# The first batch of a threshold-attention and SwiGLU kernel, issued by a planner, with k and q turned on TensorE

## The chip, the cores and the metric

The kernel runs on one core of one Trainium2 chip. The metric is the device time of one execution in microseconds (us); a profile lists every instruction of one execution, with times from the start of its span. The engines are named as in the profile: PE (TensorE; PEld is its weight load), DVE (VectorE), ACT (ScalarE), POOL (GpSimd) and SP (SyncE, which here only starts DMAs).

## What is computed

Attention with a threshold instead of a plain softmax, for 8 batches of 8 heads, 576 tokens and 64 numbers per head, and a SwiGLU block behind it, all in fp32:

```python
scores = scale * np.matmul(q, k.transpose(0, 1, 3, 2))
thresh = np.max(scores, axis=-1, keepdims=True) - tau
scores = np.where(scores >= thresh, scores, -1000000000.0)
scores = scores - np.max(scores, axis=-1, keepdims=True)
attn = np.exp(scores)
attn = attn / (np.sum(attn, axis=-1, keepdims=True) + 1e-09)
x = (attn @ v), heads side by side          # 4608 tokens x 512
g = x @ w_gate; silu = g * (1.0 / (1.0 + np.exp(-g)))
out = (silu * (x @ w_val)) @ w_out          # 512 -> 1536 -> 512
```

The three weight matrices come as 64-bit floats, 512 x 1536 twice and 1536 x 512.

## The kernel before

Work is cut by batch and by pair of heads (two heads side by side are 128 rows, 32 pairs in all). The kernel has two parts with different forms.

**The first batch** (pairs 0 to 3) is worked in tiles of 128 queries. There are 20 tiles: for each pair first the tiles 0 and 1 (here called early tiles, 8 in all), then, pair by pair in the order 3, 0, 1, 2, the tiles 2, 3 and the half tile 4 of 64 queries (the late tiles, 8 full and 4 half). A tile goes through `scores` (lines 454 to 505), `flip_steps` (514 to 549) and `attend_tile` (551 to 569):

- PE multiplies q by k for both heads into PSUM (`sc`, L463, L469 for half tiles). DVE takes the maximum (L480), ACT makes the threshold (L483, once per head) and the exponential (L484), DVE masks with the threshold and sums (L487), adds and inverts the sum (L489, L490).
- p is then divided by its sum and transposed by PE in blocks of 128 keys (`tp`, and `end` for the last 64 keys). In early tiles ACT multiplies a unit matrix by the reciprocal (L503) and PE multiplies p by this diagonal (L533, L537), which transposes and scales at once. In late tiles p itself is scaled, one head by ACT (L497) and the other by POOL (L495), and PE transposes with the plain unit matrix (L531, L539, L543).
- ACT copies the transposed p out of PSUM (L540, L544, L547), PE multiplies it by v (`xa`, L564, L566), and ACT copies the result (L569) to x.

The tile loop (766 to 824) is a pipeline written by hand: scores of tile n, then the product with v of tile n-2, then the flip of tile n-1, then other work. q and k of the pairs are loaded as blocks of 32 numbers (`load_qk`, L399), turned within 32 x 32 blocks by DVE (`prepare`, L693, L697, and L749 for the rest of q), and q is scaled before that (L403 on POOL, L696 on DVE for the first pair).

Beside the tiles the weights are converted from 64-bit words to fp32 in 24 pieces (16 of the gate and value matrices, 8 of the output matrix), each with a DMA (L314, L311), two ACT operations (L330 for the upper words, L331 for the lower), a clamp on POOL (L323), a shift and a join on DVE (L350, L356) and an addition on POOL (L366). And "plain" groups, the products of x with the gate and value weights without further tricks, fill PE: four groups of the first 256 tokens are done here (`gate`, `value`, L580; each 16 products of 128 x 128 x 256), with a multiplication on POOL (L611).

What is issued where in this part is written out by hand. `STARTS` lists the first DMAs, and `STEPS` names, for a tile by its pair and place and for a point in it, which step of the weights or of q and k is issued:

```python
STEPS = {
    (0, 0, "flipped"): ("qk",),
    (0, 1, "maxima"): ("prepare",),
    (0, 1, "masked"): ("split",),
    ...
```

**The rest** (28 pairs) runs in slots: each slot has the scores of a third of a pair (`slot_scores`, L1776) and their softmax (`slot_rest`, L1797 to L1852), every third slot a product with v (`attend`, L1873), and between them PE runs the gate, value and output products (`plain_group` L1251, `Group.mul` L1047, `outputs` L1326 and others). Their order comes from `Plan` (lines 28 to 109): every operation outside PE is a job with an engine, an estimated time, the jobs it depends on and a rank; PE's work is issued in program order with `pe`, which advances a clock `plan.t`, and whenever the clock moves, the jobs whose engine would be free are issued, lowest rank first. So the order of the instructions on each engine is fixed when the kernel is built. `PLAIN` says how many quarters of plain groups go into the slots 0 to 7, and `rest_of_weights` (905 to 944) puts the pieces not converted by then into the plan.

Of the kernel before, what the change touches and what calls it, by code (L numbers as in the profile page):

```python
# [10 lines left out]
F32 = mybir.dt.float32  # L11
# [16 lines left out]
class Plan:  # L28
# [84 lines left out]
STARTS = ("weights", "v", "weights", "qk", "weights", "v", "v", "weights")  # L113

STEPS = {
    (0, 0, "flipped"): ("qk",),
    (0, 1, "maxima"): ("prepare",),
    (0, 1, "masked"): ("split",),
    (0, 1, "end"): ("scale",),
    (1, 0, "flipped"): ("split", "shift"),  # L120
    (1, 0, "masked"): ("join",),
    (1, 1, "flipped"): ("weights 2", "prepare"),
    (1, 1, "masked"): ("split", "shift"),
    (1, 1, "end"): ("join",),
    (2, 0, "maxima"): ("rest", "weights 2"),
    (2, 0, "flipped"): ("rest",),
    (2, 0, "masked"): ("shift", "scale", "split", "join"),
    (2, 0, "end"): ("weights 2",),
    (2, 1, "maxima"): ("scale", "prepare", "v", "rest"),
    (2, 1, "flipped"): ("rest", "split"),  # L130
    (3, 0, "flipped"): ("shift",),
    (3, 0, "end"): ("join",),
    (3, 1, "maxima"): ("shift", "split", "turn last"),
    (3, 1, "flipped"): ("weights 2", "scale", "prepare"),
    (3, 1, "masked"): ("split",),
    (3, 1, "end"): ("turn", "shift", "scale"),
    (4, 0, "flipped"): ("turn", "qk"),
    (4, 1, "maxima"): ("scale",),
    (4, 1, "masked"): ("scale",),
    (4, 2, "end"): ("turn",),  # L140
# [4 lines left out]
def kernel(  # L145
# [55 lines left out]
    minus2 = const.tile([P, 1], F32, name="minus2")  # L201
    nc.vector.memset(minus2, -2.0)
# [50 lines left out]
    dbufs = deque(room(2 * P).rearrange("p (h q) -> p h q", h=2) for _ in range(2))  # L253
# [27 lines left out]
    wpieces = deque()  # L281
# [16 lines left out]
    NW = len(wpieces)  # L298
    fetched, split, used = deque(), deque(), set()
    joined = []  # L300

    def fetch_weights(n=1):
        for _ in range(n):
            if not wpieces or wpieces[0][2] in used:
                return
            dst, srcs, place = wpieces.popleft()
            used.add(place)
            m = 2 if len(srcs) == 2 else nf
            to = places[place].bitcast(U64).rearrange("p (m n) -> p m n", m=m)
            if len(srcs) == 1:  # L310
                nc.sync.dma_start(out=to, in_=srcs[0])  # L311
            else:
                for x, src in enumerate(srcs):
                    nc.sync.dma_start(out=to[:, x, :], in_=src)  # L314
            fetched.append((dst, place))

    def words(place, dst, w):
        return places[place].bitcast(U32).rearrange("p (m n w) -> p m n w", m=dst.shape[1], w=2)[:, :, :, w]

    early_slots, clamped, unclamped, shifted, unsummed = [True], [], deque(), [], []  # L320

    def clamp(eng, x):
        eng.tensor_scalar(out=x, in0=x, scalar1=1.875 * 2.0 ** -80, scalar2=2.0 ** -111, op0=ALU.min, op1=ALU.max)  # L323

    def split_weights():
        if fetched:
            dst, place = fetched.popleft()
            lo = los[0].rearrange("p (m n) -> p m n", m=dst.shape[1])
            los.rotate(1)
            nc.scalar.activation(dst, words(place, dst, 1).bitcast(F32), AF.Abs, scale=2.0 ** -96)  # L330
            nc.scalar.activation(lo, words(place, dst, 0), AF.Identity, bias=minus2, scale=-2.0 ** -51)  # L331
            unclamped.append(dst)
            if early_slots[0]:
# [1802 lines left out]
```

## Time and profile before

| What | Value |
|---|---|
| runs, median (lowest to highest) | 1362.62 us (1360.74 to 1362.79), 3 runs |
| the profiled execution | 1360.49 us |
| its span, first to last instruction | 1358.7 us |
| granted clock, mean | 1.000 |
| busy: DVE, ACT, POOL | 1065.5, 879.5, 634.8 us |
| first scores of the first batch (L463) | 7.89 us |
| third, ninth tile's scores | 16.56, 47.92 us |
| first slot's scores (L1776) | 128.80 us |
| first product with v of a slot (L1873) | 167.73 us |

The durations used below are those of the profiled execution. A row of a view with "x16" counts records: a product of fp32 operands leaves two records on PE (and two weight loads), a plain transpose one. Two instructions of one engine that follow each other can overlap by their tails, so spacing from start to start says more of PE's throughput than a mean duration. In the waits, "A <- B" means that A's engine stood idle until B ended.

### The profile page before, as it was taken

What the parts mean: (1) busy time and instruction counts of PE and PEld (TensorE: products, weight loads), DVE (VectorE), ACT (ScalarE), POOL (GpSimd) and SP (SyncE); (2) the same over time, 40 slices, a digit from 0 to 9 for tenths busy, and PEclk for the clock granted to TensorE, in tenths of its full rate; (3) what the DMA queues carried; (4) which work ended last, traced back from release to release, by engine and by line L of the source; (5) the groups of instructions that cost most, each with busy time, mean ns of one, the idle gap of its engine ahead of it and who ended that gap; (6) DMA issues with size and microseconds to landing.
All of it is one profiled execution on the core that took longest, in us unless ns stands there. A gap on an engine that the chain in (4) does not pass through costs nothing.

```text
span 1358.7 us, 39214 instructions
## 1 busy us (share of the span) xinstructions
PE 1345.4 (99%) x15590; PEld 1114.5 (82%) x15590; DVE 1065.5 (78%) x2815; ACT 879.5 (65%) x2280; POOL 634.8 (47%) x662
## 2 busy tenths in 40 slices
PE   9999999999999999999999999999999999999998
PEld 7777877887788788877887788887887788999998
DVE  7788898878887777777778777877787766788786
ACT  6888777777756767677766776777767673330330
POOL 2687497543455569324952387326932492000000
PEclk9999999999999999999999999999999999999999
DMA  8753324545425531654154514552255404424411
GB/s 187 196 183 102 73 60 136 166 132 143 140 48 162 146 92 41 190 145 114 37 172 130 157 30 136 157 141 72 65 165 145 114 27 146 155 79 146 158 60 32
DMA packets 208295, 162.33 MB, mean 119 GB/s; under 512 B 166128, under 2 KB 180464, under 8 KB 202736
## 3 DMA queue, kind: packets, MB, share of 16 engines
q1 hardware_dynamic: 204192, 158.90, 41.4%
q8 instruction: 124, 2.03, 0.6%
q10 hardware_dynamic: 3920, 0.92, 0.3%
q14 instruction: 59, 0.48, 0.1%
HBM read 138.28 MB, written 21.50 MB: 118 GB/s over the span
## 4 chain that ended last, share of the span: by engine, by line
PE 93%; DVE 3%; DMA 1%; POOL 1%; issue 0%; ACT 0%; SPq 0%; ACTq 0%; DVEq 0%; POOLq 0%
PE pb L1047 18%; PE pa L1047 12%; PE px L1529 12%; PE sc L1776 10%; PE xa L1873 9%; PE pe L1047 9%; PE po L1326 5%; PE py L1538 5%; PE pg L1251 2%; PE pv L1251 2%; PE sc L1208 2%; PE sc L463 1%; PE xa L564 1%; PE tp L533 1%; PE pe L1208 1%; PE pv L580 1%
## 5 line engine op out<-in xcount | busy, mean ns | idle before, releaser
L1824 DVE SCALAR_TENSOR_TENSOR pall<-sc,th,pall 128x288 f32<-128x288 f32 x504 | 243.9, 514 | 62.8 <-ACT pall L1822 46.1
L1047 PE MATMUL pb<-xall,big 128*128 128x256 f32 x1152 | 273.4, 380 | 0.0
L1822 ACT ACTIVATE pall<-sc,nm 128x288 f32<-128x288 f32 x504 | 231.9, 496 | 38.7 <-DVE pall L1824 38.7
L1047 PEld LDWEIGHTS pb<-xall,big 128*128 128x128 f32 x1152 | 216.9, 190 | 30.3 <-issue 2.2
L1852 DVE STREAM_TRANSPOSE pall<-pall 128x576 f32<-128x576 f32 x252 | 186.8, 761 | 29.1 <-ACT pall L1850 21.1
L1850 ACT ACTIVATE pall<-pall,ri 128x288 f32<-128x288 f32 x418 | 191.7, 527 | 24.1 <-DVE ri L1838 23.6
L1047 PE MATMUL pa<-xall,big 128*128 128x256 f32 x768 | 183.6, 382 | 0.0
L900 POOL TENSOR_TENSOR hall<-hall,tmp 128x512 f32<-128x512 f32 x80 | 102.5, 1281 | 161.2 <-DVE hall L1100 143.3
L1797 DVE TENSOR_REDUCE mx<-sc 128x2 f32<-128x576 f32 x168 | 125.5, 747 | 47.7 <-PE sc L1776 47.1
L1047 PEld LDWEIGHTS pa<-xall,big 128*128 128x128 f32 x768 | 143.2, 190 | 22.1 <-issue 3.6
L1776 PE MATMUL sc<-kT,qT 64*32 64x288 f32 (+1 forms) x5376 | 145.7, 346 | 0.9 <-issue 0.9
L1776 PEld LDWEIGHTS sc<-kT,qT 64*32 64x32 f32 x5376 | 95.6, 106 | 53.7 <-issue 19.3
L1047 PE MATMUL pe<-xall,big 128*128 128x256 f32 x576 | 137.3, 382 | 0.1
L1873 PE MATMUL xa<-pall,vall 64*32 64x288 f32 x4032 | 129.3, 404 | 0.0
L1047 PEld LDWEIGHTS pe<-xall,big 128*128 128x128 f32 x576 | 108.7, 190 | 16.9 <-issue 2.6
L1873 PEld LDWEIGHTS xa<-pall,vall 64*32 64x32 f32 x4032 | 74.1, 107 | 47.5 <-issue 6.2
L1832 ACT COPY sums<-sums 32x6 f32<-32x6 f32 x336 | 66.6, 198 | 32.4 <-DVE pall L1824 27.4
L1847 POOL TENSOR_SCALAR pall<-pall,ri 128x288 f32<-128x288 f32 x86 | 42.5, 506 | 92.6 <-DVE ri L1838 92.0
L1099 ACT ACTIVATE vall<-tmp 128x512 f32<-128x512 f32 x96 | 60.1, 629 | 31.3 <-POOL tmp L900 14.4
L900 POOL TENSOR_TENSOR tmp<-tmp 128x512 f32<-128x512 f32 x36 | 45.9, 1275 | 62.6 <-ACT tmp L1122 62.5
L1799 DVE TENSOR_REDUCE mx<-sc 128x1 f32<-128x288 f32 x168 | 75.0, 446 | 0.0
L1538 PE MATMUL py<-wo,hall 128*128 128x256 f32 x336 | 74.8, 379 | 0.0
(258 smaller groups left out, 2438.3 us busy)
## 6 DMA issues: line engine op xcount, KB each, us to landing
big<-sums_hbm SPq DMA_DIRECT2D x42, 1024.0 KB, 5.2
big<-sums_hbm SPq DMA_DIRECT2D x48, 768.0 KB, 4.8
vall<-in_v_dram SPq DMA_DIRECT2D x112, 144.0 KB, 3.1
out_dram<-big SPq DMA_DIRECT2D x32, 256.0 KB, 2.9
qT<-in_q_dram SPq DMA_DIRECT2D x112, 72.0 KB, 4.7
kT<-in_k_dram SPq DMA_DIRECT2D x112, 72.0 KB, 3.0
wo<-in_moe_w_gate_dram SPq DMA_DIRECT2D x16, 384.0 KB, 3.8
wo<-in_moe_w_val_dram SPq DMA_DIRECT2D x16, 384.0 KB, 4.5
```

The lines of the kernel that those rows point to most:

```text
L900: return lambda: nc.gpsimd.tensor_tensor(out=out, in0=a, in1=b, op=op)
L1047: nc.tensor.matmul(ps[:, i], w[:, k_, i * P:(i + 1) * P], x[:, k_, :], start=first and i == k_ == 0, stop=True, skip_group_check=True)
L1529: nc.tensor.matmul(ps, a[:, f, :], ws[n][:, f, :], start=bank_ not in begun, stop=True, skip_group_check=True)
L1538: nc.tensor.matmul(ps(), a[:, f, i * P:(i + 1) * P], operands[o][:, f, :], start=first and f == 0, stop=True, skip_group_check=True)
L1776: nc.tensor.matmul(pss[h][(slice(g * G, (g + 1) * G), *part)], qT[hs, col:col + G], kT[hs, c * SH + keys[0]:c * SH + keys[1]], start=True, ...
L1797: rs.append(job("DVE", 0.72, lambda n=n, tile_=tile_: nc.vector.tensor_reduce(out=mx[:, n:n + 2, 0], in_=tile_[:, :, 0:SH], axis=AX.X, op= ...
L1799: rs.append(job("DVE", 0.42, lambda n=n, tile_=tile_: nc.vector.tensor_reduce(out=mx[:, n + 2:n + 3, 0], in_=tile_[:, :, SH:SH + SQ], axis ...
L1822: ej = job("ACT", 0.42, lambda x=x, n=n: nc.scalar.activation(ps[x], scs[x], AF.Exp, bias=nm[:, n:n + 1]), ej, masks.get((h, u - 1)), rank=0)
L1824: masks[x] = job("DVE", 0.45, lambda x=x, n=n: nc.vector.scalar_tensor_tensor(out=ps[x], in0=scs[x], scalar=th[:, n:n + 1], in1=ps[x], op0 ...
L1850: scaled.append(job("ACT", 0.46, lambda x=x, n=n: nc.scalar.activation(x, x, AF.Copy, scale=ri[:, n:n + 1]), rj, rank=rank))
L1852: seg["turned"].append(job("DVE", 0.72, lambda both=both: nc.vector.transpose(out=both, in_=both), *scaled, rank=rank))
L1873: nc.tensor.matmul(holds[a].ap()[x * G:(x + 1) * G, 0:SH].rearrange("d (i q) -> d i q", q=G), vr[rs, h, j, ds], p[rs, h, :, j, :], start=( ...
```

## The change

The hand-written order of the first batch goes: `STEPS`, the tile loop with its points, `fetch_weights`, `split_weights`, `shift_weights`, `join_weights`, `need`, `fill`, `rest_of_weights`. `Plan`, `Bank` and `Hold` are made ahead of the first batch, and every operation of it is now a job with an estimate; `convert` makes the six jobs of a weight piece. PE's program is still one loop: scores of tile n, the extra steps that `HOOKS` names for it, the product with v of tile n-2, the flip of tile n-1, and `feed`, which adds quarters of plain groups until the account says that the masks of the tile are done. It feeds three groups; the fourth goes to slots 0 and 1, where `PLAIN` now has 6 quarters each instead of 3 and 5.

The parts that touch the arithmetic's form:

- k and q of the first batch are loaded in whole rows of 64 numbers, 128 tokens per block, and turned by PE with the unit matrix: seven transposes for each pair's k and first 256 queries (`prepare_pair`), three for the rest of q (`prepare_rest`). ACT copies them out of PSUM and scales q in the copy.
- All p of the first batch is scaled by POOL (L507 of the new kernel), both heads; ACT no longer scales p, and there are no diagonals. All flips are plain transposes (L535, L548). The keys of the second head start 64 later in every tile, so `scores` has five products in early tiles too.
- ACT makes one threshold per tile, between the two exponentials.
- The clamp of the weights is always on POOL, and the constants of the conversion differ (`plus2`, no scaling of the upper words).

```diff
-STARTS = ("weights", "v", "weights", "qk", "weights", "v", "v", "weights")
-STEPS = {
...
+STARTS = (("weights", 0), ("v", 0), ("weights", 1), ("qk", 2), ("weights", 2), ("v", 1), ("v", 2), ("weights", 3), ("qk", 3), ("v", 3))
+EARLY_PATIENCE = 0.6
+HOOKS = {
+    1: (("qk", 1), ("load", 3)),
+    2: (("load", 0),),
...
+    8: (("next", 4),),
+    10: [("rest", 0)] + [("weights", n) for n in range(16, 24)],
...
+    def convert(n, *deps):
...
+        fj = job("SP", 0.45 * len(srcs), fetch, *freed.get(place, ()), *deps, rank=1, lag=1.6, moves=2.4)
...
+        uj = job("ACT", 0.9, lambda: nc.scalar.activation(dst, up, AF.Abs), fj, *under, rank=2)
+        cj = job("POOL", 0.85, lambda: clamp(dst), uj, rank=2)
+        lj = job("ACT", 1.0, lambda: nc.scalar.activation(lo, words(place, dst, 0), AF.Identity, bias=plus2, scale=2.0 ** -51),
+                 fj, *conv[-3:-2], rank=2)
...
+        conv.append(job("POOL", 1.85, lambda: nc.gpsimd.tensor_tensor(out=ub, in0=ub, in1=lo.bitcast(U32), op=ALU.add), jj, lj, rank=2))
...
+        rj = job("DVE", 0.36, total, *masks, rank=1)
+        scaled = [job("POOL", 0.8, lambda x=x: nc.gpsimd.tensor_scalar(out=ps[x], in0=ps[x], scalar1=ri[:, x:x + 1], scalar2=1.0,
+                                                                       op0=ALU.mult, op1=ALU.mult), rj, rank=1) for x in range(m)]
...
+            def turn_keys(hold=hold, p=p, h=h):
+                tp = hold.ap()
+                for kt in range(KT):
+                    at_ = kt * P + (D * h if t < NT else 0)
+                    nc.tensor.transpose(tp[:, kt * P:(kt + 1) * P], p[:, at_:at_ + P], ident)
+            m = pe(0.45, turn_keys, *hold.deps, scaled[h])
...
+    def prepare_pair(i):
...
+        m = pe(0.45, keys, *hold.deps, landed[i, "k"])
+        kj = job("ACT", 0.53, lambda: nc.scalar.copy(kTs[i][:, 0:KM], hold.ap()), m, rank=0)
...
+        ej = job("ACT", 0.2, lambda: nc.scalar.copy(kTs[i][:, KM:S], more.ap()[:, QA:QA + D]), m, rank=0)
+        qj = job("ACT", 0.33, lambda: nc.scalar.activation(qT[:, 0:QA], more.ap()[:, 0:QA], AF.Copy, scale=scl), m, rank=0)
...
+    def feed():
+        plan.force(*last_masks)
+        until = max(j.end for j in last_masks) + 0.8
+        while fed[0] < 4 * NF2 and plan.t < until:
...
+    for n in range(len(tiles)):
+        scores(n)
+        if not n:
+            pe(1.9, lambda: run_idle(4))
+        for what, i in HOOKS.get(n, ()):
...
+        if n > 1:
+            attend_tile()
+        if n:
+            flip()
+        feed()
...
-    PLAIN = {0: 3, 1: 5, 2: 6, 3: 2, 4: 5, 5: 5, 6: 3, 7: 3}
+    PLAIN = {0: 4, 1: 6, 2: 6, 3: 2, 4: 5, 5: 5, 6: 3, 7: 3}
+    PLAIN[0] += 2 * 4 * NF2 - fed[0] - sum(PLAIN.values())
```

## The prediction

> **What bounds the kernel now.** First the page's busy line: PE is busy 99% of the span. That line cannot show a stall of half a microsecond, because the modelled end of a matmul covers it, so I split the first 168 us by stage. From PE's 160th group of instructions on (the first `xa` of L1873, at 167.73 us) the two kernels issue the same 870 groups on PE, and the list of PE's waits after 128 us holds almost nothing (0.6 us before a `pg` of L1251, 0.9 us before `sc` of L1776). So the change is worth what it does to the time of that one `xa`.
>
> ```profile
> PE 1345.4 (99%) x15590; PEld 1114.5 (82%) x15590; DVE 1065.5 (78%) x2815; ACT 879.5 (65%) x2280; POOL 634.8 (47%) x662
> ```
>
> Busy time by stage: length, then PE, PEld, DVE, ACT and POOL in us, the granted clock, DMA.
>
> ```profile
> 16.56:47.92 31.36, 31.29 (x276) 25.24 (x276) 28.75 (x63) 30.94 (x72) 15.12 (x14) 1.00 0.81 196
> 69.58:89.45 19.87, 18.52 (x141) 14.26 (x140) 15.94 (x31) 17.60 (x35) 15.57 (x11) 1.00 0.49 158
> 89.45:109.20 19.75, 18.59 (x143) 14.32 (x142) 15.74 (x30) 17.64 (x35) 16.32 (x11) 1.00 0.47 159
> 128.80:167.73 38.93, 38.35 (x437) 31.07 (x443) 34.02 (x92) 29.84 (x75) 18.28 (x19) 1.00 0.42 91
> ```
>
> The reader is to see three regimes. The first row holds the early tiles (two of each pair): ACT is busy 99%, DVE 92%. Rows two and three hold one period each of the late tiles (two full tiles, one half tile, one plain group): ACT 89%, POOL 78 to 83%, PE 93%. The last row is the first four slots: PE alone. PE's waits up to 128 us point at softmax and POOL:
>
> ```profile
> PE sc L463 <- DVE pall L487: 2.8, 4, 1.1
> ...
> PE tp L531 <- POOL big L323: 0.4, 1, 0.4
> ```
>
> **The change, part by part.** PE's pieces come from the chain of waits (start, us, what):
>
> ```profile
> 24.72 1.95 PE tp L533 x16
> 26.67 0.37 PE end L537 x4
> ...
> 119.11 0.88 PE tp L531 x8
> 119.98 0.11 PE end L539
> ...
> 128.87 1.65 PE sc L1776 x64
> ...
> 167.73 4.53 PE xa L1873 x144
> ```
>
> *Plain transposes.* An early flip now multiplies p by a diagonal, and each fp32 matmul leaves two records: 1.95 + 0.37 us. A plain transpose leaves one: 0.88 + 0.11. Eight early flips: 8 x 1.33 = 10.6 us off PE. Their scores are cut in five instead of four products: ten records take 1.30 us (69.58 to 70.88) against 1.18 (22.03 to 23.21), 8 x 0.12 = 1.0 us on.
>
> *k and q by TensorE.* 40 transposes of 0.104 us (0.83 / 8) are 4.2 us; they come in 12 blocks, each with a lead-in that the trace shows as 0.17 to 0.38 us between unlike blocks, say 0.2: 2.4 us. One pair's 0.9 us falls before the first scores. On: 5.7 us. PE's content falls by 10.6 - 1.0 - 5.7 = 3.9 us. By content it was 8 early tiles x 4.94 (22.03 to 26.97), 8 late x 3.8, 4 half tiles x 2.9, 128 plain products (55.2, with lead-ins 57.6) and 4 slot scores x 1.65: 145.7 us, of the 159.8 between the first scores (7.89) and 167.73. So 14 us are waits today, 4 of them in the first two tiles and 8 to 9 in the late ones. Both numbers are the room.
>
> *ACT.* It loses 16 diagonals of L503 (0.35 us each in a row of two), 12 scalings of L497 (0.81) and 16 of 36 thresholds (about 0.2): 5.6 + 9.7 + 3.2 = 18.5 us. It gains the copies of transposed k and q; with the rows of ACT's copies of such widths (512 columns 0.55, 128 columns 0.27) a pair costs 0.55 + 0.25 + 0.4 and its rest 0.4: 6.4 us for four. *DVE* loses the transposes of L693, L697 and L749 and one scaling, 3.0 + 1.6 + 2.0 + 0.35 = 7 us. *POOL* loses 3.6 us of scaling q and gains 28 scalings of p at 0.9 us, 25 us. Three POOL and two ACT rows:
>
> ```profile
> 24.20 1.82 POOL L366 TENSOR_TENSOR big<-big,extra 128x768 uint32<-128x768 uint32 x1
> ...
> 97.54 0.89 POOL L495 TENSOR_SCALAR pall<-pall,ri 128x576 f32<-128x576 f32 x1 [0.37 <-DVE ri L490]
> ...
> 99.30 2.52 POOL L366 TENSOR_TENSOR big<-big 128x768 uint32<-128x768 uint32 x1
> ...
> 29.38 0.70 ACT L503 ACTIVATE pall<-pall,ri 128x128 f32<-128x128 f32 x2
> ...
> 109.85 0.84 ACT L497 ACTIVATE pall<-pall,ri 128x576 f32<-128x576 f32 x1
> ```
>
> The same addition takes 1.82 or 2.52 us, the clamp of L323 0.83 or 1.53, each 0.70 longer when DVE is at its weights. The Trainium skill ("SBUF — State Buffer", section "SBUF: two separate sides") calls the port pair that GpSimd and VectorE share an exclusive lock, held for a whole instruction; these two-valued rows agree. By that rule the new scalings are blocked too, each by at most one such 0.70.
>
> *Start.* k and q arrive in rows of 64 numbers instead of 32, with fewer and larger packets; k landed at 5.7 us. But ACT issued its last start DMA only when an earlier one had landed, then loaded its table (1.28 us from 6.63), and now the copies of k and q queue behind that: 6.4 + 0.6 + 0.25 + 0.4 gives 7.7 for the first scores against 7.89. Bounds: 1.5 us earlier, 1 us later. The first softmax then sets the pace, with scores of the third tile at 16.5 as now: POOL's 0.9 for L503's 0.7 in front of the first flip, and DVE's transposes (1.2) in the second tile replaced by ACT's copies (1.2).
>
> *Early tiles.* ACT has 1.45 (two exponentials, one threshold) + 1.5 (copies) + 0.6 (k, q) + 0.9 (only half a weight piece per tile in the new order) = 4.4; DVE 3.5 + 0.8 = 4.3; PE 3.8 + 0.5 = 4.3; POOL 1.8 + 1.3. Two of six tiles have 1.1 us of copies between the two exponentials, in front of the masks. Four at 4.4, two at 5.4: 28.4 us, so the ninth tile's scores start at 45.0, now 47.9. Bounds: 42.1 (PE alone) and 47.9.
>
> *Late tiles.* The new order feeds three plain groups, not four, here; the fourth (16 products, 6.9 us) moves into the first two slots. The first three tiles carry none: 3 x 4.1 = 12.4 us, by DVE and PE. Then three periods. PE's content is 17.8 + 0.55 (rest of q) = 18.35. POOL: now 15.6 to 16.3 of 19.7 with two scalings; five make 18.3 to 19.0. ACT 17.6 - 1.6 - 0.6 + 0.4 = 15.8. POOL becomes the fullest, and each flip waits for it. I take 20.0 for a period, the nearest row being today's 19.6 to 19.9 with ACT that full; bounds 18.35 and POOL with every weight operation in its long form, 5 x 0.94 + 4 x (1.53 + 2.52) + 1.98 = 22.9. Slots start at 45.0 + 12.4 + 60.0 = 117.4, now 128.8.
>
> *Slots.* 38.9 us today for 64 products; 80 make 45.8. About five pieces of weights instead of two are joined here, some 10 us more of POOL (18.3 of 38.9 busy today) and 5 of DVE (34.0): cover enough. If it is not, PE waits a few us for masks. The sums of weights end later too, but `po` of L1326 used them at 215.8, 27 us after they were ready. SP issues fewer DMAs for k and q, and no transfer is late in either stage.
>
> **Sum.** 117.4 + 45.8 = 163.2 against 167.7: 4.5 us gained, and I add 0.5 for PE's wait of 0.6 us in the first slot, which goes: 5.0. The profiled execution took 1360.49 us (span 1358.7 and 1.8 around it); less 5.0 that is **1355.5**. The median shown is 1362.62, 2.1 above that execution, so against the median the same sum reads 1357.6.
>
> **Rivals.** *PE dense:* the new order, all on one account, runs like the slots, which wait for nothing at DVE 87%. Early tiles 4.3, periods 18.35: 42.1 + 11.2 + 55.1 + 45.8 = 154.2, 13.5 gained: 1347. Against: flips follow their softmax by 2 to 3 us, slots by 10.
> *Nothing left:* the early loop stays at 5.3 through its latency, POOL takes ACT's place: 47.9 + 12.4 + 60 + 45.8 = 166.1, 1.6 gained: 1359. For: the three engines end within 5% of each other.
> *Slower:* POOL in front of every late flip. Scaling queues behind a 2.52 us addition on an in-order engine, and the transposes stand on PE ahead of the plain products that could fill. At 22.9 a period the three cost 8.7 more than in my sum: 1364.2. It decides from 21.7 a period, where my gain is used up. Against: in most periods today half the additions are short.
> *Clock:* transposes might not count as work for the clock. 112 more of them at twice 0.104 us would add 11.6 us: 1367. The rows against it: 80 transposes ran at 0.104 us and the granted clock is 1.00 in every stage. The Trainium skill ("TensorE: Matmul & The Clock Gate", section "Part 4: PE-mode transpose") says that the full clock does not engage for transposes; no row here shows that.
>
> **Chances.** Forecast 0.42 (its own range 1352 to 1358), PE dense 0.22, nothing left 0.22, slower 0.11, clock 0.03. A measurement of this kernel tells about 0.2% (2.7 us) from no change, so faster means below 1357.8. Faster: 0.39 + 0.22 + 0.04 = 0.65; slower: 0.01 + 0.09 + 0.03 = 0.13; the same 0.22. The range, 1346 to 1364, leaves out half the slower case, the clock, and the far end of PE dense.
>
> **What would show it.** The first slot scores (L1551) start near 117 and the first `xa` of L1648 near 163; early tiles follow at 4.4 to 5.4; transposes keep 0.104 us and clock 1.00; POOL is over 90% busy in the late tiles and ends PE's waits before `tp`. I am wrong if the early loop stays at 5.3, if PE waits in the first slots, or if POOL's scalings take much over 0.9.

## The result, and the profile after

Five runs of the changed kernel: 1367.84 us median (1366.24 to 1368.69), against 1362.62 (1360.65 to 1363.20) of the kernel before on the same chip: ratio 1.0042, 95% interval 1.0027 to 1.0057. It is slower by 0.4%, some 5 us; the forecast was 1355.5 (1357.6 beside the median). The profiled execution took 1367.84 us (span 1366.0, mean granted clock 0.994); that of the kernel before lies at the fast end of its runs (1360.49), so between the two profiles the difference is 7.3 us.

The page's busy line has not moved, and the stages have. First that line, then the view by stage (length, then PE, PEld, DVE, ACT, POOL, granted clock, DMA), here the early tiles, the three late periods, and the slots up to the first `xa` of L1648:

```profile
PE 1346.7 (99%) x15550; PEld 1115.9 (82%) x15550; DVE 1072.2 (78%) x2800; ACT 873.5 (64%) x2252; POOL 656.4 (48%) x685
```

```profile
15.99:45.08 29.09, 28.72 (x240) 22.92 (x240) 25.00 (x55) 25.63 (x57) 15.90 (x18) 1.00 0.62 157
58.07:77.14 19.07, 18.54 (x145) 14.00 (x144) 15.98 (x26) 15.93 (x33) 13.01 (x12) 1.00 0.72 248
77.14:102.47 25.33, 21.90 (x144) 16.49 (x143) 19.85 (x36) 16.91 (x32) 19.25 (x15) 0.87 0.44 128
102.47:126.04 23.57, 20.29 (x141) 15.01 (x141) 19.02 (x32) 15.99 (x31) 22.25 (x18) 0.86 0.18 65
126.04:175.72 49.68, 45.61 (x461) 37.27 (x461) 46.85 (x102) 38.58 (x86) 34.44 (x28) 1.00 0.49 119
```

The early tiles are faster than before. One late period is good (19.1 us), the next two take 25.3 and 23.6 us, with a granted clock of 0.87 and 0.86, where the kernel before had 1.00. In the slots VectorE is busy 46.9 of 49.7 us. The list of PE's waits (us in total, times, longest) has three new entries at its head:

```profile
PE end L548 <- ACT xlast L577: 4.1, 2, 3.0
PE xa L1648 <- issue: 3.5, 1, 3.5
PE xa L570 <- DVE hall L623: 2.3, 1, 2.3
```

The rows of PE's timeline that answer to those shown of before (start, us, what): a plain flip, the first slot, the first `xa` of the slots.

```profile
99.61 1.10 PE L535 MATMUL tp<-pall 128*128 128x128 f32 x8
...
126.04 1.72 PE L1551 MATMUL sc<-kT,qT 64*32 64x288 f32 x64
...
175.72 0.84 PE L1648 MATMUL xa<-pall,vall 64*32 64x288 f32 x6 [3.46 <-issue]
```

The first `xa` starts at 175.72 instead of 167.73, 8.0 us later; the span is 7.3 us longer. So nothing more was lost behind it, and all of the loss lies ahead of it.

**Where it was lost.** The second late period shows it. VectorE's timeline, then GpSimd's, then PE's:

```profile
73.88 2.16 DVE L398 TENSOR_SCALAR big<-big 128x768 uint32<-128x768 uint32 x1 [0.72 <-POOL big L371]
76.08 1.46 DVE L400 SCALAR_TENSOR_TENSOR big<-wo,big 128x768 uint32<-128x768 uint32 x1
77.46 0.80 DVE L496 SCALAR_TENSOR_TENSOR pall<-sc,th,pall 128x576 f32<-128x576 f32 x1
...
78.58 1.27 DVE L398 TENSOR_SCALAR big<-big 128x768 uint32<-128x768 uint32 x1
79.89 1.38 DVE L400 SCALAR_TENSOR_TENSOR big<-wo,big 128x768 uint32<-128x768 uint32 x1
81.19 0.67 DVE L623 SCALAR_TENSOR_TENSOR hall<-tmp,pv 128x512 f32<-128x512 f32 x1
81.79 1.41 DVE L489 TENSOR_REDUCE nm<-sc 128x1 f32<-128x576 f32 x2
```

```profile
73.81 1.81 POOL L402 TENSOR_TENSOR big<-big 128x768 uint32<-128x768 uint32 x1
75.60 1.13 POOL L371 TENSOR_SCALAR big<-big 128x768 f32<-128x768 f32 x1
77.62 1.81 POOL L402 TENSOR_TENSOR big<-big,extra 128x768 uint32<-128x768 uint32 x1 [0.89 <-DVE big L400]
79.53 0.93 POOL L507 TENSOR_SCALAR pall<-pall,ri 128x576 f32<-128x576 f32 x1
```

```profile
77.14 2.54 PE L467 MATMUL sc<-pall 64*128 64x288 f32 x10
82.01 1.97 PE L570 MATMUL xa<-big,vall 128*64 128x128 f32 x16 [2.33 <-DVE hall L623]
```

The shift of a weight piece (L398) takes 0.54 us when GpSimd stands. Here it begins 0.07 us behind an addition of GpSimd (73.81 to 75.62), takes 2.16 us and ends 0.42 us after that addition. The shift at 78.58 takes 1.27 us and again ends 0.42 us after GpSimd's addition. The join (L400) goes from 0.95 to 1.38 and 1.46. So one side stands still while the other runs. The masks of L496, whose scores lie in PSUM, keep 0.81 us throughout. Two conversions now stand in VectorE's queue ahead of the gate's product (L623), which PE's `xa` waits for. The Trainium skill ("SBUF — State Buffer", section "SBUF: two separate sides") says that an instruction of VectorE with two SBUF inputs or in a two-port mode, and one of GpSimd, exclude each other as a whole. These rows agree.

The other two long waits begin on VectorE too. Its rows, ScalarE's and PE's ahead of the wait of 3.0 us, then VectorE's last transposes of p ahead of the first `xa` of the slots:

```profile
112.05 1.30 DVE L400 SCALAR_TENSOR_TENSOR big<-wo,big 128x768 uint32<-128x768 uint32 x1
113.28 1.41 DVE L489 TENSOR_REDUCE nm<-sc 128x1 f32<-128x576 f32 x2
...
114.06 0.74 ACT L491 ACTIVATE pall<-sc,nm 128x576 f32<-128x576 f32 x1 [2.23 <-DVE nm L489]
116.02 0.21 ACT L577 COPY xlast<-xa 128x64 f32<-128x64 f32 x1
...
116.29 0.47 PE L548 MATMUL end<-pall 128*128 128x128 f32 x1 [3.02 <-ACT xlast L577]
...
174.21 1.41 DVE L1627 STREAM_TRANSPOSE pall<-pall 128x576 f32<-128x576 f32 x2
```

Two joins and a shift (110.11 to 113.35) stand ahead of the maxima at 113.28. ScalarE's exponential waits 2.23 us for these, the copy L577 stands behind it on ScalarE, and PE waits for the copy. For the first `xa` of the slots the list names no releaser; in the kernel that product depends on the transposes of L1627, and the last of them ends at 175.62, 0.1 us ahead of it. Two shifts and a join of weights (168.08 to 171.56), and maxima behind these, stand ahead of them on VectorE.

Then comes a second price. The same 16 records of `xa` take 1.09 us at 103.77 and 1.97 here. The stages in steps of half a microsecond show where (the granted clock is the third number from the end):

```profile
80.50:81.00 0.50, 0.00 (x0) 0.00 (x0) 0.50 (x1) 0.00 (x0) 0.00 (x0) 0.53 1.00 406
87.00:87.50 0.50, 0.50 (x3) 0.41 (x2) 0.39 (x1) 0.50 (x2) 0.50 (x1) 0.65 0.00 0
```

The clock is at 0.50 from 80.53 to 87.35, from 114.66 to 121.49 and from 176.10 to 179.5 (a mean of 0.53 over half a microsecond is 0.50 from 0.03 us on), and each stretch begins in or just behind one of the three long waits.

### The profile page after: what moved, and what is told of

It reads as the page before. It is cut to its first block, busy times and chain, and to the rows that moved or that the text cites. A ratio compares the mean times of both kernels' runs of the same rounds, so it can differ in the third digit from the quotient of the medians.

```text
span 1366.0 us, 39121 instructions
## 1 busy us (share of the span) xinstructions
PE 1346.7 (99%) x15550; PEld 1115.9 (82%) x15550; DVE 1072.2 (78%) x2800; ACT 873.5 (64%) x2252; POOL 656.4 (48%) x685
## 3 DMA queue, kind: packets, MB, share of 16 engines
q1 hardware_dynamic: 196304, 158.90, 40.9%
q8 instruction: 123, 2.02, 0.6%
## 4 chain that ended last, share of the span: by engine, by line
PE 93%; DVE 5%; issue 1%; ACT 1%; DMA 0%; POOL 0%; SPq 0%; DVEq 0%; ACTq 0%; POOLq 0%
PE pb L861 18%; PE pa L861 12%; PE px L1304 12%; PE sc L1551 10%; PE xa L1648 9%; PE pe L861 9%; PE po L1101 5%; PE py L1313 5%; PE pv L602 2%; PE pg L602 2%; PE sc L1022 2%; PE sc L467 1%; DVE big L400 1%; PE pe L1022 1%; DVE pall L496 1%
## 5 line engine op out<-in xcount | busy, mean ns | idle before, releaser
L1627 DVE STREAM_TRANSPOSE pall<-pall 128x576 f32<-128x576 f32 x252 | 186.8, 761 | 29.8 <-ACT pall L1625 22.0
L359 POOL TENSOR_TENSOR hall<-hall,tmp 128x512 f32<-128x512 f32 x84 | 108.1, 1287 | 158.8 <-DVE hall L914 141.8
L1648 PE MATMUL xa<-pall,vall 64*32 64x288 f32 x4032 | 130.7, 408 | 3.5 <-issue 3.5
L1648 PEld LDWEIGHTS xa<-pall,vall 64*32 64x32 f32 x4032 | 77.0, 108 | 49.4 <-issue 9.1
```

What stands on the lines that cost most here:

```text
L359: return lambda: nc.gpsimd.tensor_tensor(out=out, in0=a, in1=b, op=op)
L1627: seg["turned"].append(job("DVE", 0.72, lambda both=both: nc.vector.transpose(out=both, in_=both), *scaled, rank=rank))
L1648: nc.tensor.matmul(holds[a].ap()[x * G:(x + 1) * G, 0:SH].rearrange("d (i q) -> d i q", q=G), vr[rs, h, j, ds], p[rs, h, :, j, :], start=( ...
```

## The experiments

Times are medians beside the kernel before on the same chip. PE starts cold in some executions (last section), so stages are counted from the ninth tile's scores. "Late" is from there to the first slot, "slots" from there to the first `xa` of the slots. The number of plain products in each of the two differs where the order differs, so the sum is what compares. The kernel before took 1361.1 to 1361.6 us (medians) on the chips of the experiments; the ratio is over all executions, so that a single one that is some us longer draws it away from the ratio of the medians.

| kernel | late, us | slots, us | sum | time, us | ratio to before (interval) |
|---|---|---|---|---|---|
| before | 80.9 | 38.9 | 119.8 | 1362.62 | 1 |
| forecast | 72.4 | 45.8 | 118.2 | 1357.6 | |
| changed | 81.0 | 49.7 | 130.6 | 1367.84 | 1.0042 (1.0027 to 1.0057) |
| keep_clock | 76.9 | 51.2 | 128.1 | 1365.70 | 1.0043 (1.0025 to 1.0060) |
| no_dve_weights | 69.5 | 45.0 | 114.5 | 1348.90 | 0.9908 (0.9894 to 0.9923) |
| no_pool_scale | 73.3 | 49.7 | 123.1 | 1361.42 | 1.0002 (0.9993 to 1.0012) |
| no_add_scale | 69.6 | 47.2 | 116.8 | 1356.45 | 0.9962 (0.9948 to 0.9976) |
| act_head0 | 62.8 | 75.8 | 138.6 | 1375.04 | 1.0100 (1.0085 to 1.0115) |
| dve_scale | 64.4 | 78.3 | 142.7 | 1380.98 | 1.0144 (1.0129 to 1.0159) |
| true_account | 65.5 | 66.3 | 131.8 | 1366.98 | 1.0047 (1.0029 to 1.0064) |
| lock_plan | 56.9 | 87.5 | 144.4 | 1382.56 | 1.0154 (1.0139 to 1.0169) |
| xlast_first | 65.3 | 62.9 | 128.2 | 1366.61 | 1.0047 (1.0029 to 1.0065) |
| late_wo | 79.1 | 49.4 | 128.5 | 1368.28 | 1.0039 (1.0024 to 1.0053) |
| late_wo_clock | 76.9 | 50.5 | 127.4 | 1364.90 | 1.0027 (1.0016 to 1.0037) |
| ep2 | 83.0 | 48.2 | 131.2 | 1368.47 | 1.0051 (1.0036 to 1.0066) |
| ep2_late | 81.5 | 48.1 | 129.6 | 1368.00 | 1.0050 (1.0033 to 1.0066) |
| before_pool_all | 83.3 | 39.8 | 123.1 | 1365.30 | 1.0026 (1.0017 to 1.0035) |
| before_plain | 81.0 | 39.0 | 120.0 | 1361.14 | 0.9998 (0.9989 to 1.0007) |

The theory at the start: VectorE comes late because its weight operations run long beside GpSimd's, and the clock doubles the price of each long wait. The rivals: GpSimd with all scalings is itself too full; ScalarE's queue order; the account's durations; the clock falls because of the transposes.

**keep_clock: is it the gap that takes the clock?**

```diff
-            marks.append(pe(..., (lambda h=h: one(h)) if full else both_heads, *deps))
+            marks.append(pe(..., (lambda h=h: one(h, 4 if h and k == 14 else 1)) if full else both_heads, *deps))
...
-                for kt in range(KT):
+                for kt in list(range(KT)) * (7 if h and len(flipped) == 18 else 1):
...
-                for c in range(NCC):
+                for c in list(range(NCC)) * (2 if (t, g, mat, i) == (1, 1, 1, 1) else 1):
```

> Same order on every engine as the changed kernel; only in the three stretches in which PE stood for about 3 us (before the xa of tile 12, before the end of tile 17, before the first xa of the slots) the matmuls just before are issued again into the same bank: second head of the 15th tile's scores four times, one flip's four transposes seven times, one plain product twice. More work on PE, nothing less. Theory 'gap, then half clock': the granted clock stays 1.00 through 180 us, slots start at 119 to 121 instead of 126.0, first xa of the slots near 169 instead of 175.7, time 1360 to 1362. Rival 'the clock falls for another reason (transposes, load)': drops to 0.66 to 0.83 stay, time 1368 or a little more.

PE's timeline, the repeated scores, and the two stages:

```profile
77.04 5.80 PE L467 MATMUL sc<-pall 64*128 64x288 f32 x28
```

```profile
44.98:121.85 76.87, 74.44 (x581) 57.67 (x581) 65.75 (x117) 59.17 (x117) 60.47 (x50) 1.00 0.46 142
121.85:173.06 51.21, 47.93 (x469) 38.62 (x469) 48.50 (x104) 38.54 (x86) 36.85 (x30) 1.00 0.48 116
```

The clock stays at 1.00, and with more work on PE the slots start at 121.85 instead of 126.04. So the late tiles' two drops cost 4.1 us of their length, and it is the wait that brings them, not the transposes, of which there are 24 more here. Of this, 2.5 us are left in the sum (first `xa` at 173.06; 169 was expected). The slots, with VectorE busy 48.5 of 51.2 us, take back the rest. The time misses the expected 1360 to 1362 us, and the timed ratio (1.0043; by the medians 1.0031, as one of six executions took 1372.12) doesn't resolve a gain.

**no_dve_weights, no_pool_scale, no_add_scale: which side is too full?** All three keep the changed kernel's order on every engine, and shrink instructions to 8 columns, so that most of that work is left out. In no_dve_weights GpSimd's addition is one of floats, in full width (1.82 us, the same as clear in the changed kernel). In no_add_scale the clamps stay on GpSimd.

```diff
-        sj = job("DVE", 0.6, lambda: nc.vector.tensor_scalar(out=ub, in0=ub, scalar1=3, ...), cj, rank=2)
-        jj = job("DVE", 1.0, lambda: nc.vector.scalar_tensor_tensor(out=ub, ...), sj, rank=2)
+        sj = job("DVE", 0.6, tiny, cj, rank=2)
+        jj = job("DVE", 1.0, tiny, sj, rank=2)
```

> Leaves out part of the weights: shift and join run on 8 columns of 384 instead of all, and GpSimd's addition is one of floats, so the weights are wrong; the order on every engine is that of the changed kernel. VectorE loses some 45 us of 144 before the first xa of the slots. Theory 'VectorE comes late to maxima and masks because of its weight operations': none of the three waits of 3 us is left, no drop of the clock, slots start at 117 to 120, first xa of the slots at 162 to 165, time 1354 to 1357. Rival 'ScalarE's order or GpSimd's scalings hold PE': at least two of the three waits stay, time over 1363.

```diff
-        scaled = [job("POOL", 0.8, lambda x=x: nc.gpsimd.tensor_scalar(out=ps[x], in0=ps[x], ...
+        scaled = [job("POOL", 0.8, lambda x=x: nc.gpsimd.tensor_scalar(out=ps[x][:, :, 0:8], in0=ps[x][:, :, 0:8], ...
```

> Leaves out most of the scaling of p (GpSimd scales 8 columns of 576 of each head), so p stays unscaled; the order on every engine is that of the changed kernel, VectorE has all of its weight work. Theory 'VectorE's shift and join stand still while a GpSimd instruction runs, and the other way round': shift and join come down from 0.87 and 1.43 us to about 0.70 and 1.15 (what is left comes from additions and clamps), VectorE loses some 10 us without having less to do, first xa of the slots at 163 to 166, time 1354 to 1358. Rival 'the weight operations are too many for VectorE, whatever GpSimd does': means stay within 0.08 us, time over 1362.

```diff
-        conv.append(job("POOL", 1.85, lambda: nc.gpsimd.tensor_tensor(out=ub, in0=ub, in1=lo.bitcast(U32), op=ALU.add), ...
+        conv.append(job("POOL", 1.85, lambda: nc.gpsimd.tensor_tensor(out=dst[:, :, 0:8], in0=dst[:, :, 0:8], in1=lo[:, 0:dst.shape[1], 0:8], op=ALU.add), ...
(and the scaling as in no_pool_scale)
```

> Leaves out most of GpSimd's scalings of p and of its additions (8 columns each; the clamp's bound is 2 to the -10 and the shift is by 0, so that the unfinished weights stay small): p is unscaled and the weights are wrong. VectorE has all of its weight instructions in full width, in the order of the changed kernel. Theory 'blocking': shift and join run near their clear 0.55 and 0.95 us, no wait over 2 us, slots to first xa under 47 us, first xa at 160 to 164, time 1350 to 1355. Rival 'VectorE's content': with 36 us of weight work still on VectorE the slots take 49 us again and the time is that of no_pool_scale, 1360 or more.

The two stages of no_dve_weights, then of no_add_scale (columns as above):

```profile
44.65:114.13 69.48, 66.56 (x539) 51.10 (x539) 46.38 (x118) 59.01 (x117) 52.64 (x52) 1.00 0.43 140
114.13:159.10 44.97, 44.96 (x462) 36.87 (x461) 36.79 (x101) 37.98 (x86) 31.16 (x29) 1.00 0.55 131
```

```profile
48.93:118.50 69.57, 66.64 (x539) 51.31 (x538) 56.43 (x118) 58.98 (x117) 29.51 (x51) 1.00 0.51 157
118.50:165.73 47.23, 44.96 (x461) 36.87 (x461) 43.30 (x102) 37.90 (x86) 22.90 (x29) 1.00 0.52 125
```

The groups of shift and join up to the first `xa`, for the 16 pieces in `big`: changed kernel first, then no_add_scale (busy us, mean ns).

```profile
L400 DVE SCALAR_TENSOR_TENSOR big<-wo,big 128x768 uint32<-128x768 uint32 x16 | 23.3, 1457 | 0.6 <-issue 0.3
L398 DVE TENSOR_SCALAR big<-big 128x768 uint32<-128x768 uint32 x16 | 13.9, 876 | 0.7 <-POOL big L371 0.7
```

```profile
L400 DVE SCALAR_TENSOR_TENSOR big<-wo,big 128x768 uint32<-128x768 uint32 x16 | 16.9, 1055 | 0.3
L398 DVE TENSOR_SCALAR big<-big 128x768 uint32<-128x768 uint32 x16 | 10.0, 628 | 0.0
```

Take VectorE's share of the pair away, and the sum is 114.5 us with GpSimd's work complete. Take GpSimd's share away, and it is 116.8 us with VectorE's instructions complete. So neither engine's own content sets the 130.6 us: each fits alone, below the forecast's 118.2, and the two together do not. On VectorE the difference is standing still: from the ninth tile to the first `xa` the same instructions keep it busy 112.8 us (65.97 + 46.85) in the changed kernel and 99.7 in no_add_scale, so 13.1 us. On GpSimd it is 12.8 us: 96.6 in the changed kernel and 83.8 in no_dve_weights, again with its instructions in full width. The runs do not show how much of this lies on PE's path, because the shrunk instructions also end sooner themselves. GpSimd's scaling takes 0.75 us in no_dve_weights and 0.93 in the changed kernel.

The expectations were not all met. no_dve_weights is 5 us faster than the range I gave. no_add_scale took 1356.45 where 1350 to 1355 was expected, its slots 47.2, and a wait of 2.3 us stays ahead of its first `xa`. no_pool_scale took 1361.42 where 1354 to 1358 was expected, between its two theories. Its join falls to 1.19 us, as blocking said, and its late tiles shrink to 73.3 us. But the slots keep 49.7 and the shift keeps 0.89 us: the other instructions of GpSimd, additions, clamps and gates, are still there. A longest wait of 3.5 us stays.

**act_head0, dve_scale: another engine for the scalings.**

```diff
-        scaled = [job("POOL", 0.8, lambda x=x: nc.gpsimd.tensor_scalar(out=ps[x], ...
+        scaled = [job("ACT", 0.81, lambda x=x: nc.scalar.activation(ps[x], ps[x], AF.Copy, scale=ri[:, x:x + 1]), rj, rank=1)
+                  if x == 0 and m > 1 and k >= NP * TA else
+                  job("POOL", 0.8, ...
```

> Only the 8 scalings of p of the first head in the late full tiles go back to ScalarE (0.81 us each); all else is planned by the same rules. Rival 'GpSimd with all scalings is the cause': VectorE's shift and join come down from 0.87 and 1.43 us to 0.60 and 1.10, at least two of the waits go, time 1358 to 1361. Theory 'VectorE has too much weight work put in these tiles whoever scales': means fall by under 0.1 us, waits of 2 us and more stay, time 1364 to 1369.

```diff
-        scaled = [job("POOL", 0.8, lambda x=x: nc.gpsimd.tensor_scalar(
+        scaled = [job("DVE" if late else "POOL", 0.42 if late else 0.8, lambda x=x: (nc.vector if late else nc.gpsimd).tensor_scalar(
```

> In the late tiles VectorE scales p instead of GpSimd (20 scalings, put in the account at 0.42 us by the rate of the shift, 0.54 us for 768 columns). VectorE gets 8.4 us more to do, GpSimd 15 us less. If it is the mutual blocking that costs: shift and join come down to 0.7 and 1.2, VectorE's busy time stays or falls in spite of the 8.4 us, time 1358 to 1363. If it is VectorE's plain content: VectorE's busy time up by 8 us, time 1370 or more.

Both are slower than the changed kernel (1375.04 and 1380.98 us). act_head0 lies outside what either theory gave. dve_scale came out as its second theory said: 1370 us or more, and VectorE is busy 9.1 us longer (1081.3 for 1072.2 over the whole span). PE's waits, act_head0 first, then dve_scale:

```profile
PE xa L574 <- ACT big L556: 7.5, 7, 1.8
```

```profile
PE pg L604 <- POOL big L402: 8.8, 2, 7.3
```

In act_head0 the shift comes down to 0.70 us for the pieces in `big`, but over all 24 pieces only from 0.87 to 0.80 us, and the join from 1.43 to 1.33; PE now waits for ScalarE's copies. The order moved too: the planner fed the late tiles no plain group in act_head0 and one and a quarter in dve_scale, where the changed kernel has three. In dve_scale 5 pieces are joined there instead of 12, and PE stood 8.8 us for finished weights (L402). So relieving GpSimd by itself was no cure here. As the order moved with the engine, these two do not separate the theories.

**true_account, lock_plan, xlast_first: the order by another account.**

```diff
-        sj = job("DVE", 0.6, ...      +        sj = job("DVE", 0.87, ...
-        jj = job("DVE", 1.0, ...      +        jj = job("DVE", 1.43, ...
-        cj = job("POOL", 0.85, ...    +        cj = job("POOL", 0.93, ...
-        scaled = [job("POOL", 0.8,    +        scaled = [job("POOL", 0.93,
```

> Only the durations in the account are set to the means that the trace of the changed kernel shows: shift 0.87 for 0.60, join 1.43 for 1.00, clamp 0.93 for 0.85, scaling 0.93 for 0.80; the planner then orders by them (it feeds fewer plain products in the late tiles). Theory 'the order is bad because the account thinks VectorE is free earlier than it is': the long waits shrink to under 2 us, no or one drop of the clock, time 1360 to 1364. Rival 'the order is the same whatever the numbers, there is simply too much work there': time 1366 to 1370.

```diff
+    def open_at(self, j):
+        return max(j.ready, self.free["POOL"]) if j.lock else j.ready
...
+        if j.lock:
+            self.free["POOL"] = max(self.free["POOL"], self.free[e])
...
+        sj.lock = jj.lock = True
```

> Only the account is changed: it lets a shift or join begin only when GpSimd is free by the account, and GpSimd begin nothing while one runs; the same instructions, ordered by that. If the loss comes from an order that puts shift and join beside GpSimd's instructions: their means fall to 0.65 and 1.1, no wait over 2 us, time 1356 to 1362. If the two together have too much to do in that stage whatever the order: the means fall but the sums of weights come later, PE waits for them in the slots, time 1364 to 1372.

```diff
-        j = job("ACT", 0.25, lambda: nc.scalar.copy(to, hold.ap()[:, 0:n]), m, rank=1)
+        j = job("ACT", 0.25, lambda: nc.scalar.copy(to, hold.ap()[:, 0:n]), m, rank=0)
```

> Only the copies of the products with v on ScalarE (0.25 us, 20 of them) get the first rank, so that none queues behind the exponentials of the next tile; the planner orders the rest by that. Theory 'VectorE late': PE's waits for the bank of that copy (4.1 us in two places) go but appear as waits for masks or scalings; time 1364 to 1369. Rival 'ScalarE's queue order is the cause': time 1357 to 1361.

PE's first waits in true_account, then in lock_plan:

```profile
PE pg L602 <- POOL big L402: 8.1, 1, 8.1
```

```profile
PE pg L609 <- POOL big L409: 15.2, 5, 4.2
```

With true durations or with the exclusion in the account, the planner puts less into the late tiles: two plain groups and one instead of three, 9 and 6 joins instead of 12 (first slot at 110.5 and 101.8 us). Then the plain products of the slots wait for weights that are not converted. true_account's time (1366.98) lies in its rival's range, with shift and join at 0.91 and 1.47 us. xlast_first moves the order the same way (two and a half groups, first slot at 111.4, 5.1 us of such waits). Shift and join did not get shorter in lock_plan (1.06 and 1.26 us for the pieces in `big`), so its greedy rule does not keep the two apart on the chip, and it failed as a test of a better order. The ScalarE rival gets no support: the waits for the copy of L577 are no longer on xlast_first's list, and the time stays. It is not excluded, since the order of plain products and conversions changed with it.

**late_wo, ep2, ep2_late, late_wo_clock: conversions later, or earlier.**

```diff
-        uj = job("ACT", 0.9, ..., rank=2)    (and cj, lj, sj, jj and the addition)
+        uj = job("ACT", 0.9, ..., rank=3 if n >= NW * 2 // 3 else 2)
```

> Only the rank of the conversion of the last 8 pieces (the output weights) is lowered from 2 to 3, so that in the first slots they stand behind the scaling and the transposes of p until they are 12 us old. Same instructions. Theory 'the first slots take 49.7 us because VectorE has 30 us of softmax and 18 us of conversions there': late tiles as in the changed kernel (slots from 126), slots to first xa 46 to 48 us, the wait of 3.5 us ahead of that xa goes, time 1363 to 1366. Rival 'the slots wait for something else': 49 to 50 us again, time as the changed kernel. Rival 'given back later': xa earlier, but PE waits for sums of output weights after 200 us.

```diff
-EARLY_PATIENCE = 0.6
+EARLY_PATIENCE = 0.2
```

> Only EARLY_PATIENCE is 0.2 for 0.6: an engine of the first batch no longer keeps itself free for 0.6 us for a softmax step to come, so conversions get in earlier (12 joins ahead of the 29th maximum instead of 9, 19 instead of 15 ahead of the last one). Theory 'conversions come too late and pile up in the late tiles and slots': early tiles up to 2 us longer, slots shorter (46 to 48 us), fewer long waits, time 1362 to 1366. Rival 'each conversion costs its time wherever it stands, and softmax steps behind it are late': late tiles longer still, time 1368 to 1375.

ep2_late has both edits; late_wo_clock has that of late_wo and the first two of keep_clock.

> Both of the former: EARLY_PATIENCE 0.2, and rank 3 for the conversion of the output weights. If each acts in its own stage, the gains add: slots at 46 us, time 1359 to 1364. If they share one cause (VectorE over its account in the first slots), the sum is no better than the better one.

> The kernel with rank 3 for the output weights, and in the two waits of 3 us of the late tiles the matmuls just before issued again (second head of the 15th tile's scores four times, one flip's four transposes seven times), as in keep_clock. If the clock's price (4.2 us at the start of the slots) is kept once VectorE does not take it back: slots from 121 to 122, first xa at 168 to 169, time 1359 to 1362. If it is taken back: within 1 us of late_wo.

late_wo takes the wait ahead of the first `xa` from 3.5 to 0.8 us, but a new one of 1.5 us appears earlier in the slots, followed by 3.4 us at half clock (147.2 to 150.6): 49.4 us again, so the gain expected there did not come. Three of its five executions took 1368.28 to 1368.63 us, the other two 1364.30 and 1364.84; the profiled one is of the longer kind, and its ninth tile starts 4 us later than in the changed kernel (last section). ep2 shortens the slots to 48.2 and lengthens the late tiles to 83.0: the rival of that run, each conversion costs where it stands. The two together gain no more than about 1 us on the changed kernel's sum. late_wo_clock has the least sum among the complete relatives of the changed kernel (127.4 us, 1.0027) and is still slower than before. Its sum is 1.1 us under that of late_wo, so of the 2.2 us that its late tiles gain the slots take back half. The 3.4 us between the two medians are mostly the start: the two shorter executions of late_wo are as fast as late_wo_clock. No complete version that I tried is faster than the kernel before.

**before_pool_all, before_plain: one part of the change alone, in the old order.**

```diff
-                if x % 2:
+                if True:
                     nc.gpsimd.tensor_scalar(out=ps[x], in0=ps[x], scalar1=ri[:, x:x + 1], ...
```

> The kernel before with one part of the change alone: in the late tiles GpSimd scales the first head too (12 scalings taken from ScalarE), in the old order written out by hand. If all scalings on GpSimd are what costs by itself: late tiles 1 to 2 us a period longer, time 1365 to 1372. If it costs only together with the new order: within 2 us of before, 1359 to 1364.

```diff
-        return TA <= t < NT
+        return t < NT
...
-        if t >= TA:
+        if True:
             for x in range(m):
-                if x % 2:
+                if x % 2 or t < TA:
...
-        if t < TA:
+        if False:
             units = [dbufs[0][:, x, :] for x in range(m)]
```

> The kernel before with the other part alone: the early tiles scaled by GpSimd and turned by plain transposes (5 products of scores for 4), nothing else. By the prediction's own rows PE loses 10.6 us and gets 1.0, ScalarE loses 5.6 us in the early loop. If the early loop follows: ninth tile's scores up to 2 us earlier, time 1359 to 1362. If the loop is bound by the latency of its softmax: no difference, 1361 to 1364; GpSimd's longer scaling (0.9 for 0.43) in front of the flip may even cost 1 to 2 us.

PE's waits in before_pool_all:

```profile
PE sc L463 <- DVE pall L487: 4.1, 4, 1.7
PE tp L531 <- POOL pall L495: 3.0, 5, 0.9
```

With all late scalings on GpSimd the old kernel loses 0.26% (0.17 to 0.35), 3.5 us; its first `xa` starts 3.3 us later, at 171.04, and its flips wait for GpSimd. But VectorE's shifts and joins hardly stretch there. Their busy time up to the first `xa` (an estimate from their clear durations of 0.54 and 0.95 us is 34 to 35 us):

| | GpSimd scales one head of the late tiles | both heads | 8 columns of both heads |
|---|---|---|---|
| old order | 38.5 us (before) | 40.9 us (before_pool_all) | |
| new order | | 53.7 us (changed; early tiles too) | 48.7 us (no_pool_scale) |

So in the old order the scalings cost time mainly by holding up flips. The stretching comes mostly with the new order, even when the scalings are shrunk. How the changed kernel's 0.42% divides between the two is not shown: the 0.26% was measured in the other order, and in the new one leaving out the scalings gives back all of the loss (1.0002).

With plain transposes in the early tiles alone the old kernel is the same (0.9998), and its ninth tile starts at 48.40, not earlier than 47.92. PE's waits for masks (L487) grow from 2.8 to 7.1 us there, and a stretch of half clock appears, from 19.04 to 22.45.

## Why the prediction was wrong

- **Common point: right.** Span and first `xa` moved by 7.3 and 8.0 us. The first `xa` was forecast at 163.2 and came at 175.72, 12.5 us later: 8.0 of this are in the three late periods, 3.9 in the slots and 0.6 in the first three late tiles.
- **Plain transposes, and k and q on PE: durations right, worth wrong.** In the chain of waits the eight transposes of a flip take 0.87 us and the end 0.11, at clock 1.00 (0.88 and 0.11 forecast). But before_plain shows that 10.6 us off PE in the early tiles gain nothing in the old order: PE waits for the masks instead.
- **Early tiles: 45.0 forecast, 45.08 measured; part of the gain was a loan.** The tiles from the third on follow at 4.1 to 5.4 us, as forecast (4.4 and 5.4). But I counted "half a weight piece per tile" as relief of ScalarE and did not ask where the other half goes. Up to 48 us ScalarE's copies of weights were these (before, then changed):

```profile
L330 ACT ACTIVATE big<-wo 128x768 f32<-128x768 f32 x6 | 5.8, 968 | 0.0
L331 ACT ACTIVATE big<-wo,minus 128x768 f32<-128x768 uint32 x4 | 4.3, 1066 | 0.0
L331 ACT ACTIVATE extra<-wo,minus 128x768 f32<-128x768 uint32 x2 | 2.1, 1072 | 0.0
```

```profile
L394 ACT ACTIVATE big<-wo 128x768 f32<-128x768 f32 x4 | 3.7, 926 | 0.0
L396 ACT ACTIVATE big<-wo,plus 128x768 f32<-128x768 uint32 x2 | 2.1, 1036 | 0.0
L396 ACT ACTIVATE extra<-wo,plus 128x768 f32<-128x768 uint32 x1 | 1.1, 1063 | 0.0
```

  12.2 us against 6.9, so 5.3 us of ScalarE's work moved to later stages. On VectorE one join and three shifts moved with it, 2.6 us at their clear durations.
- **Late tiles: this step failed.** "I take 20.0 for a period": the three took 19.1, 25.3 and 23.6 us, two of them above the upper bound of 22.9, and together 8.0 us more than the 60.0 of the sum. I had the collision in hand (the two-valued rows of GpSimd), but I priced it on GpSimd only, "each by at most one such 0.70". It also stretches VectorE's shift and join, from 0.54 and 0.95 us clear to means of 0.87 and 1.43. The kernel before shows it too, in single rows (one join of 2.02 us, with means of 0.59 and 1.09), and I did not price it. And the bound left out the half clock, 4.1 us by keep_clock. GpSimd was not the fullest throughout: 68, 76 and 94% busy in the three periods, where I named over 90%.
- **Slots: "cover enough" failed.** I put five pieces there and 5 us on VectorE. Eight were joined there, and shift and join took 18.0 us, where the kernel before had 4.0 (for three joins, not the two that I took). VectorE was busy 46.9 of 49.7 us, its standing still included: longer than the forecast's 45.8.
- **Rivals.** "Slower" named the right conflict and the wrong place: PE waited 0.3 us for GpSimd's scaling before `tp`, and 9.9 us in the three entries at the head of the list. Of these, 4.7 us stay in no_add_scale (2.2 for the copy of L577, 2.3 ahead of the first `xa`, 0.2 for L623), so about half goes with GpSimd's scalings and additions. "Clock" was given the wrong cause. Transposes ran at clock 1.00 for the first 80 us; the half clock follows waits.

## What to carry to other kernels

Where one engine's instructions exclude another's, add the two up as one resource before you move work onto either; the busy time of each by itself will look free. How to order work by that is open here: lock_plan tried it with a greedy rule and lost. When a stage gets faster because work was left out of it, find the stage that has to do it, and price it there with the durations that hold beside its new neighbours. And a wait of PE of a few us can be priced twice: count the half clock behind it.

## What the runs showed of the hardware

The half clock comes in stretches of one length or a multiple of it: 6.83, 6.83 and 3.41 us in the changed kernel, four of 3.41 us in late_wo (from 20.92, 85.78, 119.91 and 147.22), and one of 13.65 us in dve_scale (from 145.38). And its beginnings lie on a grid: 114.66 - 80.53 = 34.13 = 10.0 x 3.413, 176.10 - 114.66 = 61.44 = 18.0 x 3.413, and in late_wo 64.86 = 19.0 x 3.413, 34.13 = 10.0 x 3.413 and 27.31 = 8.0 x 3.413. So a clock of its own decides, every 3.41 us, and the length of a wait alone does not: 1.5 us of standing brought the half clock in late_wo_clock (pv at 141.94, half clock from 142.2), 1.7 us did not in keep_clock (ahead of 173.06). The Trainium skill ("TensorE: Matmul & The Clock Gate", section "Part 1: The HAM clock gate (the \"warmup\" mystery)") describes a free-running window of 3413 ns, and these rows agree; its threshold of one idle window is more than the 1.5 us here. Its section "Part 4: PE-mode transpose" says that the full clock doesn't engage for transposes; here eight took 0.87 us at clock 1.00 (from 123.40 in the changed kernel) and four 0.85 us at 0.50 (from 84.71), which speaks against it, though they ran among other matmuls.

The same window may be what shows at the start, which I had not expected. In the profiled executions of late_wo and no_add_scale PE was still slow at the first scores; PE's timeline of late_wo:

```profile
7.71 2.51 PE L467 MATMUL sc<-pall,qT 64*128 64x288 f32 x10 [0.68 <-ACT qT L693]
10.15 3.78 PE L260 MATMUL idle<-pall 128*128 128x256 f32 x8
13.86 1.46 PE L467 MATMUL sc<-pall,qT 64*128 64x288 f32 x10
```

In the changed kernel the same rows take 1.36 and 1.99 us, and the ninth tile starts 4 us earlier. The profile's granted clock shows 1.00 in both up to 20.9 us, so at the start only the durations tell. In late_wo and no_add_scale the first stretch at 0.50 follows at 20.9 us; the changed kernel has none there. The kernel before issues 12 records of idle matmuls ahead of its first scores, these issue 8; whether that decides it was not tried.
